# Moving small sums between engines in a fused layer: segment sums on TensorE, memory queries normalised at every step

## The chip, the cores and the metric

The kernel runs on one core of a Trainium2 chip. The metric is device time in microseconds. The kernel before takes 1494.43 us (median of three runs, 1494.37 to 1498.48). The profile describes one execution, whose span from first to last instruction is 1492.6 us; all times inside the kernel are counted from the start of that span.

A core has five engines that work side by side, each on its own queue of instructions: TensorE (PE: matrix products, whose weight loads are shown apart as PEld), VectorE (DVE), ScalarE (ACT), GpSimd (POOL) and SyncE (SP, used here to issue transfers). TensorE writes its products into PSUM; VectorE and ScalarE read them from there ("evict" them), and only then can TensorE use the same PSUM tile again.

## The reference

The input x is 2048 tokens of 1024 channels in bf16. After a layer norm it feeds two branches, whose sums with x are the output.

```python
# A: attention in 64 segments of 32 tokens, with 8 memory tokens carried along
for s in range(64):
    h = concat([mem, xn[32*s : 32*s + 32]])           # 40 tokens
    q, k, v = h @ Wq, h @ Wk, h @ Wv                  # 32 heads of 128
    p = softmax(where(mask, q @ k.T * scale, -1e9))
    o = (p @ v) @ Wo
    mem = o[:8]                                       # for the next segment
    out_A[s] = o[8:]
# B: mixing MLP
h  = gelu(layernorm(xn) @ w1)                         # 1024 x 1024
x1 = xn + shift(h) @ w2                               # tokens shifted by +-1, +-2
out_B = x1 + gelu(layernorm(x1) @ w3) @ w4            # 1024 -> 3584 -> 1024
out = x + out_A + out_B
```

The memory runs from segment to segment, which would make branch A serial. The kernel instead assumes that a memory query attends evenly to its 40 keys, so that the next memory follows from the **sum** of a segment's tokens. It computes these 64 segment sums early, sends them through Wv and Wo in advance, and then handles four blocks of 16 segments in parallel. Along the way it computes what the memory queries really yield, compares that with what it had assumed, and at the end runs a slow exact loop if they differ. With these inputs that loop isn't entered.

## The kernel before

The stages of the program, with the tile sizes: 16 tiles of 128 tokens; blocks ("tb" in the MLP, "b" in attention) of 512 tokens; 32 attention steps, each one block and four heads.

Statistics and first normalisation of a tile (VectorE and GpSimd), then transposes by TensorE or by a transposing transfer, then the product with w1:

```python
def ln_half(n, c):                       # c = 0, 1: half of the channels
    nc.vector.bn_stats(sts[n][:, c, :], xts[n][:, c*512:(c+1)*512])
    if c == 0: return
    nc.vector.bn_aggr(lnst[:, n, 0:2], sts.pop(n)[:])
    nc.vector.tensor_scalar(ab[:, 0:1], lnst[:, n, 1:2], EPS, None, op0=add)
    nc.vector.tensor_scalar(ab[:, 1:2], ab[:, 0:1], EPS, lnst[:, n, 1:2], op0=mult, op1=add)
    nc.gpsimd.tensor_tensor(lnst[:, n, 2:4], ab[:], neghalf[:], op=pow)
    ...                                  # loads of later x tiles
def ln_apply(n):
    nc.vector.tensor_scalar(xn2[:], xts[n][:], mean, rstd2, op0=subtract, op1=mult)
    ...
def normalise_x(n):                      # xts[n] becomes the normalised x, in place
    nc.scalar.activation(xts[n][:], xts[n][:], Identity, bias=..., scale=...)

warm(12); ln_stats(0); ln_half(1, 0); ln_apply(0); pe_trans(0)
ln_half(1, 1); w1_first(0, range(4)); ...
ln_half(2, 0); ln_apply(1); pe_trans(1)
...                                      # [cut] tiles 1 to 5
for g in range(2, 8):                    # pairs of tiles
    for n in (2*g + 2, 2*g + 3): ln_stats(n + 1); ln_apply(n); dma_trans(n)
    stage1(g, range(4))                  # 4 chains of 8 matmuls, 256 columns
    for n in (2*g, 2*g + 1): normalise_x(n)
    stage1(g, range(4, 8))
```

The MLP's second part, per block tb: 28 chains of 8 matmuls into h3T, then 4 tiles x 2 halves, each a chain of 28 matmuls and one VectorE eviction into R1. Between the chains a "filler" does the segment sums (blocks 0 and 1) and the products of the sums with 16 weight chunks (4 heads each; first Wv, then Wo):

```python
def make_xn(n):                          # normalised x to DRAM, 256 KB
    nc.sync.dma_start(xt[:], x_v[:, n, :])
    nc.vector.tensor_scalar(xt[:], xt[:], mean, rstd, op0=subtract, op1=mult)     # L455
    nc.gpsimd.dma_start(xn_v[:, n, :], xt[:])
def load_sum(b):                         # 512 tokens back, transposed
    nc.sync.dma_start_transpose(sums[b], xn_d[b*512:(b+1)*512, :])
def seg_sums(b, k0):
    nc.vector.tensor_reduce(xs[:, k0:k0+2, 16*b:16*b+16], sums[b]..., op=add)     # L463
plan[(1, 1, 2*i + 1)] = i                # chunk i after half 2i+1 of block 1, and so on
def load_R1(n):                          # residual of tile n
    nc.sync.dma_start(R1[:], R1_v[:, n, :]); nc.sync.dma_start(xt[:], x_v[:, n, :])
    nc.gpsimd.tensor_tensor(R1[:], R1[:], xt[:], op=add)

for tb in range(4):
    for f in range(28):
        ... 8 matmuls (L580), gelu by ScalarE; filler(tb, 0, f)
        if f == 20: load_R1(4*tb)
    for j in range(4):
        if j < 3: load_R1(4*tb + j + 1)
        for ch in range(2):
            ps = mm_tile("ps4")          # one of four PSUM tiles, in turn
            ... 28 matmuls (L596)
            nc.vector.tensor_tensor(R1[...], ps[:], R1[...], op=add)              # L597
            filler(tb, 1, 2*j + ch)
        nc.gpsimd.dma_start(R_v[:, n, :], R1[:])
        if tb == 3 and j == 0: att_prep()        # first attention weights, 4 MB
```

Attention: in step i TensorE makes queries, keys and values (4 chains each), the scores of step i-1 and the values of step i-2. The softmax runs on VectorE; column 32 of the scores is the memory query, whose probabilities are used unnormalised and divided once per block:

```python
def soft(s):
    ...                                  # 2 transposes, mask, sum, reciprocal, product (VectorE)
    nc.vector.transpose(s.PT[:, :, 0:SEG], Pn[:])                                 # L707
    nc.gpsimd.tensor_copy(s.PT[:, :, SEG:W], ET[:, :, SEG:W])                     # memory column
    ...
    nc.gpsimd.tensor_copy(EMs[s.b][...], ET[...][:, :, :, SEG])
def norm_sums(b):                        # once per block
    for j in range(4): nc.tensor.matmul(psN[:, j, :], qones[:, j, :], EM, ...)    # 128x128
    nc.vector.tensor_scalar(rm, psN, float(M), None, op0=add)
def norm_recip(b, j): nc.vector.reciprocal(rms[b][:, j, :], rms[b][:, j, :])
def norm_apply(b): nc.vector.tensor_tensor(o4, o4, rms[b]..., op=mult)
def norm_add(b):   nc.vector.tensor_tensor(oTs[b][:], oTs[b][:], VM[...], op=add)
def out_part(b, c, h0, h1, nsp=1):       # output chain: 32 matmuls per part, nsp equal parts
    ...
# end of the kernel
norm_sums(b); norm_recip x4; norm_apply(b); norm_add(b); compare(b); finite()
out_chain(b, 4); out_chain(b, 5); out_chain(b, 6); verdict(); out_part(b, 7, 0, 32, 2)
```

Of the kernel before, what the change touches and what calls it, by code (L numbers as in the profile page):

```python
# [29 lines left out]
H = 32  # L30
# [33 lines left out]
def kernel(  # L64
# [37 lines left out]
    def const_tile(name, arr, dt=BF16, later=False):  # L102
        a = _bf(arr) if dt == BF16 else np.asarray(arr, np.float32)
        d = nc.inline_tensor(a, name=name)
        t = cpool.tile(list(arr.shape), dt, name=name + "_sb")
        load = lambda: nc.gpsimd.dma_start(t[:], d.ap())
        if later:
            return load, t
        load()
        return t  # L110
# [36 lines left out]
    m0s = spec.tile([P, KT, 1], F32)  # L147
# [17 lines left out]
    with ExitStack() as keepx:  # L165
# [6 lines left out]
        with ExitStack() as p0:  # L172
# [29 lines left out]
            def ln_half(n, c):  # L202
                if c == 0:
                    sts[n] = ring.tile([P, 2, 6], F32, tag="st", name="st")
                nc.vector.bn_stats(sts[n][:, c, :], xts[n][:, c * 512:(c + 1) * 512])  # L205
                if c == 0:
                    return
                nc.vector.bn_aggr(lnst[:, n, 0:2], sts.pop(n)[:])
                ab = ring.tile([P, 2], F32, tag="ab", name="ab")
                nc.vector.tensor_scalar(ab[:, 0:1], lnst[:, n, 1:2], EPS, None, op0=ALU.add)  # L210
                nc.vector.tensor_scalar(ab[:, 1:2], ab[:, 0:1], EPS, lnst[:, n, 1:2], op0=ALU.mult, op1=ALU.add)
                nc.gpsimd.tensor_tensor(lnst[:, n, 2:4], ab[:], neghalf[:], op=ALU.pow)
                for t in {0: (3,), 1: (4, 5), 2: (6, 7)}.get(n, (n + 5,)):
                    if t < NT:
                        load_x(t)
# [9 lines left out]
            def ln_apply(n):  # L225
                g, j = divmod(n, 2)
                if j == 0:
                    xn2Ts[g] = ring.tile([P, 2, KT, P], BF16, tag="xn2T", name="xn2T", bufs=4)
                xn2 = xn2s[n] = ring.tile([P, D], BF16, tag="xn2", name="xn2", bufs=4)
                nc.vector.tensor_scalar(xn2[:], xts[n][:], lnst[:, n, 0:1], lnst[:, n, 3:4], op0=ALU.subtract, op1=ALU.mult)  # L230
                nms[n] = ring.tile([P, 1], F32, tag="nm", name="nm", bufs=8)
                nc.gpsimd.tensor_scalar(nms[n][:], lnst[:, n, 0:1], lnst[:, n, 2:3], -1.0, op0=ALU.mult, op1=ALU.mult)
# [14 lines left out]
            def pe_trans(n):  # L247
                xn2 = xn2s.pop(n)
                ps = [mm_tile("psT")[:], mm_tile("psT")[:]]
                for h in range(2):  # L250
                    p3_ = ps[h].rearrange("p (k t) -> p k t", k=4)
                    for k in range(4):
                        nc.tensor.matmul(p3_[:, k, :], xn2[:, (4 * h + k) * P:(4 * h + k + 1) * P], ident[:], start=True, stop=True)
                    for q in range(0, 4, 2 if n == 0 else 4):
                        w = 2 if n == 0 else 4
                        nc.scalar.copy(xn2Ts[n // 2][:, n % 2, 4 * h + q:4 * h + q + w, :], p3_[:, q:q + w, :])

# [42 lines left out]
            load_eye9()  # L300
# [19 lines left out]
            ln_stats(5)  # L320
            ln_apply(4)
            dma_trans(4)
            single(3, 0)
            normalise_x(2)
# [5 lines left out]
            for g in range(2, NT // 2):  # L330
# [7 lines left out]
                for n in (2 * g, 2 * g + 1):  # L338
                    normalise_x(n)
                stage1(g, range(4, KT))  # L340

# [5 lines left out]
        with ExitStack() as p2:  # L347
            ring = p2.enter_context(tc.tile_pool(name="p2ring", bufs=4))
            for n in range(NT):
# [23 lines left out]
                if n == 8:  # L373
                    load_qones()
                    load_causal()
                    load_mask40()

    attx = main.enter_context(ExitStack())
    with ExitStack() as p3:
# [12 lines left out]
        nc.vector.tensor_copy(m0s[:], ps9[:, :, M:M + 1])  # L392
# [49 lines left out]
        for i in range(4):  # L442
            plan[(1, 1, 2 * i + 1)] = i
            plan[(2, 0, 7 * i + 6)] = 4 + i
            plan[(2, 1, 2 * i + 1)] = 8 + i
            plan[(3, 0, 7 * i + 6)] = 12 + i
# [3 lines left out]
        sums = {}  # L450

        def make_xn(n):
            xt = ring.tile([P, D], BF16, tag="xt", name="xt", bufs=2)
            nc.sync.dma_start(xt[:], x_v[:, n, :])
            nc.vector.tensor_scalar(xt[:], xt[:], lnst[:, n, 0:1], lnst[:, n, 2:3], op0=ALU.subtract, op1=ALU.mult)  # L455
            nc.gpsimd.dma_start(xn_v[:, n, :], xt[:])

        def load_sum(b):
            sums[b] = x3_pool.tile([P, KT * 512], BF16, tag="x0", name=f"xTs{b}")
            nc.sync.dma_start_transpose(sums[b][:].rearrange("p (k t) -> p k t", k=KT), xn_d[b * 512:(b + 1) * 512, :])  # L460

        def seg_sums(b, k0):
            nc.vector.tensor_reduce(xs[:, k0:k0 + 2, 16 * b:16 * b + 16], sums[b][:].rearrange("p (k s i) -> p k s i", k=KT, i=SEG)[:, k0:k0 + 2, :, :], axis=AX.X, op=ALU.add)  # L463

        def last_sum():
            nc.vector.tensor_tensor(xb[:, :, 0:1], m0s[:], xs[:, :, 0:1], op=ALU.add)
            nc.vector.tensor_copy(xb[:, :, 1:NG], xs[:, :, 1:NG])
            load_chunk(0, 0)

        prep = {}  # L470

        def do(tb, ph, i, f, *a):
            prep.setdefault((tb, ph, i), []).append((f, a))

        for n in range(6):
            do(0, 0, 10 + 3 * n, make_xn, n)
        for n in range(6, 14):
            do(0, 1, n - 6, make_xn, n)
        do(1, 0, 0, make_xn, 14)
        do(1, 0, 3, make_xn, 15)  # L480
        for b, (load, sumat) in enumerate((((0, 1, 1), [(0, 1, 4)] * 4), ((0, 1, 5), [(1, 0, 1)] * 2 + [(1, 0, 2)] * 2),
                                           ((1, 0, 3), [(1, 0, 10 + t) for t in range(4)]), ((1, 0, 14), [(1, 0, 22 + t) for t in range(4)]))):
            do(*load, load_sum, b)
            for t, pos in enumerate(sumat):
                do(*pos, seg_sums, b, 2 * t)
        do(1, 0, 26, last_sum)

        def filler(tb, ph, i):
            for f, a in prep.get((tb, ph, i), ()):
                f(*a)  # L490
# [13 lines left out]
        def load_R1(n):  # L504
# [4 lines left out]
            nc.gpsimd.tensor_tensor(R1[:], R1[:], xt[:], op=ALU.add)  # L509
            R1s[n] = R1  # L510
# [47 lines left out]
        def att_prep():  # L558
# [14 lines left out]
            nc.gpsimd.memset(A["SS"][:], 0.0)  # L573

        for tb in range(4):
            for f in range(FT):
# [6 lines left out]
                if f == 20:  # L583
                    load_R1(tb * 4)
            if tb == 3:
                rightx.close()
                att_open()
# [30 lines left out]
    EMs = {}  # L618
# [6 lines left out]
    def new_step(i):  # L625
# [4 lines left out]
        if s.hg == 0:  # L630
            EMs[s.b] = smp.tile([P, NHG, 4, 4], BF16, tag="EM", bufs=2, name="EM")
# [64 lines left out]
    def soft(s):  # L696
# [11 lines left out]
        nc.gpsimd.tensor_copy(s.PT[:, :, SEG:W], ET[:, :, SEG:W])  # L708
# [4 lines left out]
        nc.gpsimd.tensor_copy(EMs[s.b][:, s.hg, :, :].rearrange("p h m -> p m h"), ET[:].rearrange("p (m h) i -> p m h i", h=4)[:, :, :, SEG])  # L713
# [77 lines left out]
    rms = {}  # L791

    def norm_sums(b):
        ps = mm_tile("psN")
        p3_ = ps[:].rearrange("p (j c) -> p j c", j=4)
        EM = EMs[b][:].rearrange("p g h m -> p (g h m)")
        for j in range(4):
            nc.tensor.matmul(p3_[:, j, :], qones[:, j, :], EM, start=True, stop=True)
        rm = smp.tile([P, 512], F32, tag="rm", name="rm")
        rms[b] = rm[:, 0:512].rearrange("p (j c) -> p j c", j=4)  # L800
        nc.vector.tensor_scalar(rms[b], p3_, float(M), None, op0=ALU.add)

    def norm_recip(b, j):
        nc.vector.reciprocal(rms[b][:, j, :], rms[b][:, j, :])

    def norm_apply(b):
        o4 = oTs[b][:].rearrange("p h (m j) -> p h m j", j=4)
        nc.vector.tensor_tensor(o4, o4, rms[b].rearrange("p j (h m) -> p h m j", m=4), op=ALU.mult)

    def norm_add(b):  # L810
# [39 lines left out]
    def out_part(b, c, h0, h1, nsp=1):  # L850
        m, ch = divmod(c, 2)
        w = 512 // nsp
        if h0 == 0:
            parts[b, c] = [mm_tile("psP") for _ in range(nsp)]
        for q in range(nsp):
            ps = parts[b, c][q]
            cc = slice(ch * 512 + q * w, ch * 512 + (q + 1) * w)
# [7 lines left out]
            nc.vector.tensor_tensor(ot[:, 0:w], ps[:, 0:w], Rt[:, q * w:(q + 1) * w], op=ALU.add)  # L865
# [24 lines left out]
    for i in range(NS):  # L890
# [29 lines left out]
        if s.hg == 2 and s.b > 0:  # L920
            at(2, norm_sums, s.b - 1)
            for j in range(4):
                at((4, 5, 7, 8)[j], norm_recip, s.b - 1, j)
            at(10, norm_apply, s.b - 1)
            at(11, norm_add, s.b - 1)
# [34 lines left out]
        if last:  # L960
# [17 lines left out]
            norm_sums(b)  # L978
            for j in range(4):
                norm_recip(b, j)  # L980
            norm_apply(b)
            norm_add(b)
# [6 lines left out]
            out_part(b, 7, 0, H, 2)  # L989
# [129 lines left out]
```

## Time and profile before

| stretch (us) | what runs there | length | TensorE busy | VectorE busy | ScalarE busy |
|---|---|---|---|---|---|
| 0 to 68.73 | layer norm, transposes, product with w1 | 68.73 | 63.34 | 36.55 | 44.78 |
| 68.73 to 124.36 | product with w2, second layer norm | 55.63 | 55.31 | 46.26 | 18.42 |
| 124.36 to 221.07 | MLP block 0 | 96.71 | 96.45 | 13.79 | 18.46 |
| 221.07 to 333.70 | MLP block 1 | 112.63 | 103.41 | 30.36 | 16.72 |
| 333.70 to 438.10 | MLP block 2 | 104.40 | 104.08 | 7.63 | 16.72 |
| 438.10 to 538.80 | MLP block 3 | 100.70 | 100.44 | 10.38 | 16.72 |
| 538.80 to 765.00 | attention, block 0 | 226.20 | 224.45 | 94.89 | 76.05 |
| 765.00 to 1492.60 | attention, blocks 1 to 3, and the end | 727.60 | 720.11 | 284.62 | 137.47 |

How to read it: the rows come from the busy times of each engine in windows of the trace. A row's length less the busy time of TensorE is the time in which TensorE did nothing. Some matmul records are missing, and in a long row they show as a little idle time. A line of the profile that is shown below names the engine, the line of the kernel (L597), the operation, what it wrote and read, the shape, how often it ran, and, in brackets, for how long the engine had been idle before it and what ended that. The granted clock is TensorE's, as a share of full speed.

### The profile page before, as it was taken

The numbers are of one execution on the slowest core, as the hardware profiler recorded it, in microseconds if no ns is written. First come the engines' busy times: TensorE is split into PE (matmuls) and PEld (weight loads), VectorE is DVE, ScalarE is ACT, GpSimd is POOL, SyncE is SP. The second block draws the span as 40 slices with busy tenths as digits, with TensorE's granted clock in tenths as the row PEclk, the third lists the DMA queues.
The fourth block names the chain that finished last, engine by engine and source line by source line (L and its number), as shares of the span: only waits on it lengthen the run. The fifth ranks groups of instructions, "written<-read, shape, count | busy, mean of one in ns | idle before, by whom it ended". The sixth has DMA issues, their size and how long they took to land.

```text
span 1492.6 us, 27953 instructions
## 1 busy us (share of the span) xinstructions
PE 1467.6 (98%) x12154; PEld 755.3 (51%) x12272; DVE 524.5 (35%) x1042; ACT 345.3 (23%) x871; POOL 205.7 (14%) x482
## 2 busy tenths in 40 slices
PE   8999997999999999999999999999999999999998
PEld 7844443444444456666544444444444444444444
DVE  8283034110000212445440355431264442163443
ACT  5633202203103013333320222220123220032220
POOL 6152131121211101121200000000000000000000
PEclk9999999999999999999999999999999999999999
DMA  8599765342542634565532364451245442244301
GB/s 218 138 266 226 280 216 151 118 153 96 191 149 99 212 113 157 183 190 180 184 114 64 94 174 150 143 169 49 83 142 171 155 156 72 67 142 147 123 12 62
DMA packets 207999, 216.77 MB, mean 145 GB/s; under 512 B 66936, under 2 KB 174600, under 8 KB 207872
## 3 DMA queue, kind: packets, MB, share of 16 engines
q1 hardware_dynamic: 199584, 187.21, 42.2%
q0 software_dynamic: 8288, 27.72, 5.4%
q8 instruction: 98, 1.61, 0.5%
q14 instruction: 29, 0.24, 0.1%
HBM read 174.26 MB, written 25.17 MB: 134 GB/s over the span
## 4 chain that ended last, share of the span: by engine, by line
PE 94%; DMA 2%; DVE 2%; issue 1%; SPq 1%; POOL 0%; DVEq 0%; POOLq 0%
PE psK L659 15%; PE psP L859 15%; PE psV L668 15%; PE psQ L641 15%; PE ps L580 13%; PE ps L596 11%; PE ps L356 4%; PE ps L260 2%; PE psS L692 1%; PE psO L722 1%; PE psM L677 1%; DMA xt<-in_A_x_dram 1%; DVE st L205 1%; PE psvb L414 1%; PE psG L435 1%
## 5 line engine op out<-in xcount | busy, mean ns | idle before, releaser
L859 PE MATMUL psP<-wo_sb,oX 128*128 128x512 bf16 (+1 forms) x1035 | 221.1, 372 | 1.1
L596 PE MATMUL ps<-w,hT_all 128*128 128x512 bf16 x874 | 193.7, 379 | 1.2
L659 PEld LDWEIGHTS <-w 128*128 128x128 bf16 x1280 | 125.1, 98 | 99.1
L641 PE MATMUL psQ<-xT,w 128*128 128x512 bf16 x744 | 169.1, 379 | 1.3
L668 PE MATMUL psV<-w,xT 128*128 128x512 bf16 x744 | 169.0, 379 | 1.3
L659 PE MATMUL psK<-xT,w 128*128 128x512 bf16 x763 | 169.4, 379 | 0.3
L859 PEld LDWEIGHTS <-oX 128*128 128x128 bf16 x1056 | 103.1, 98 | 117.2
L641 PEld LDWEIGHTS <-w 128*128 128x128 bf16 x1024 | 98.7, 98 | 116.0
L660 ACT CAST K<-psK 128x512 bf16<-128x512 f32 (+1 forms) x160 | 80.2, 501 | 303.8 <-PE psK L659 302.8
L648 DVE TENSOR_TENSOR Q<-psQ,QM 128x512 bf16<-128x512 f32 (+1 forms) x128 | 87.2, 685 | 166.0 <-PE psQ L641 107.5
L669 ACT CAST V<-psV 128x512 bf16<-128x512 f32 x128 | 74.8, 584 | 289.7 <-PE psV L668 289.6
L596 PEld LDWEIGHTS <-hT_all 128*128 128x128 bf16 x896 | 87.2, 98 | 103.8
L581 ACT ACTIVATE hT_all<-ps 128x512 bf16<-128x512 f32 x112 | 66.7, 597 | 294.9 <-PE ps L580 294.9
L668 PEld LDWEIGHTS <-xT 128*128 128x128 bf16 x768 | 74.1, 98 | 84.7
L580 PE MATMUL ps<-xn3T,w3a 128*128 128x512 bf16 x448 | 100.9, 387 | 8.9 <-DVE R L597 8.9
L580 PE MATMUL ps<-xn3T,w3b 128*128 128x512 bf16 x448 | 97.7, 379 | 0.0
L727 DVE TENSOR_TENSOR oX<-psE,VM 128x128 bf16<-128x128 f32 x32 | 9.3, 291 | 215.3 <-PE psE L723 215.3
L734 DVE TENSOR_TENSOR oX<-psO,VM 128x96 bf16<-128x96 f32 (+2 forms) x256 | 82.0, 391 | 0.0
L865 DVE TENSOR_TENSOR ot<-psP,Rt 128x512 bf16<-128x512 f32 (+1 forms) x33 | 22.3, 675 | 167.7 <-PE psP L859 164.9
L580 PEld LDWEIGHTS <-w3a 128*128 128x128 bf16 x448 | 44.1, 99 | 63.2 <-issue 13.3
L597 DVE TENSOR_TENSOR R<-ps,R 128x512 f32<-128x512 f32 x32 | 22.0, 689 | 137.8 <-PE ps L596 137.2
L580 PEld LDWEIGHTS <-w3b 128*128 128x128 bf16 x448 | 43.6, 98 | 51.9
(160 smaller groups left out, 1252.4 us busy)
## 6 DMA issues: line engine op xcount, KB each, us to landing
w<-in_A_Wq_dram SPq DMA_DIRECT2D x32, 1024.0 KB, 5.4
w<-in_A_Wk_dram SPq DMA_DIRECT2D x32, 1024.0 KB, 5.5
w<-in_A_Wv_dram SPq DMA_DIRECT2D x32, 1024.0 KB, 6.4
R_scratch<-x POOLq DMA_DIRECT2D x16, 512.0 KB, 9.0
xt<-in_A_x_dram SPq DMA_DIRECT2D x32, 256.0 KB, 3.8
R<-R_scratch SPq DMA_DIRECT2D x16, 512.0 KB, 6.4
R_scratch<-R POOLq DMA_DIRECT2D x16, 512.0 KB, 6.4
chunk<-in_A_Wv_dram SPq DMA_DIRECT2D x8, 1024.0 KB, 5.6
```

Of the source, the lines that this page charges most:

```text
L356: nc.tensor.matmul(ps[:], hTB[:, k, o:o + P], w2_sb[:, k, ch * 512:(ch + 1) * 512], start=(k == 0), stop=(k == KT - 1))
L580: nc.tensor.matmul(ps[:], w3[:, k, (f % FH) * P:(f % FH + 1) * P], xn3Ts[tb][:, :, k, :], start=(k == 0), stop=(k == KT - 1))
L581: nc.scalar.activation(h3T[:, f, :], ps[:], ACTF.Gelu_apprx_tanh)
L596: nc.tensor.matmul(ps[:], h3T[:, f, j * P:(j + 1) * P], w4t[f // 4][:, f % 4, ch * 512:(ch + 1) * 512], start=(f == 0), stop=(f == FT - 1))
L641: nc.tensor.matmul(ps[:], w[:, k, hh * P:(hh + 1) * P], s.xm[:, k, 0:512], start=(k == 0), stop=(k == KT - 1))
L648: nc.vector.tensor_tensor(q3[:, j0:16, 0:SEG], p3_[:, j0:16, :], QM[:, 4 * s.hg + hh, z + j0:z + 16].unsqueeze(2).to_broadcast((P, 16 - j0 ...
L659: nc.tensor.matmul(ps[:, 0:c], w[:, k, hh * P:(hh + 1) * P], s.xm[:, k, h2 * c:(h2 + 1) * c], start=(k == 0), stop=(k == KT - 1))
L660: nc.scalar.copy(s.K[:, hh, h2 * c:(h2 + 1) * c], ps[:, 0:c])
L668: nc.tensor.matmul(ps[:], s.xm[:, k, m * P:(m + 1) * P], w[:, k, :], start=(k == 0), stop=(k == KT - 1))
L669: nc.scalar.copy(s.V[:, m, :], ps[:])
L734: nc.vector.tensor_tensor(oX[:, h0:h0 + hn, :].rearrange("p h (m c) -> p m h c", c=P)[:, m0:m1, :, SEG * j:SEG * (j + 1)], o4[:, 4 * m0:4 ...
L859: nc.tensor.matmul(ps[:, 0:w], oX[:, h, m * P:(m + 1) * P], wo_sb[:, h, cc], start=(h == 0), stop=(h == H - 1))
```

## The change

Five things are moved.

1. **Segment sums** are made by TensorE in the first stage, straight from the normalised tiles in SBUF: the tile is the weight, and a constant of 128x4 (which token belongs to which of the tile's four segments) is the moving operand, eight matmuls of four columns a tile. ScalarE copies the result. This replaces the sums by VectorE from a transposed copy read back from DRAM. The normalised x that attention reads from DRAM is now made in the residual's load, from the x that is loaded there anyway. The products with the weight chunks move earlier by half a block.
2. **Memory queries** are normalised in every step: their 16 probabilities per partition are transposed so that their sum lies along the free axis, summed, divided, transposed back and put into the probabilities that the values are multiplied with. The sums by TensorE and the divisions once per block fall away.
3. **Tile 0** is normalised in two pieces, of 256 and 768 channels, so that its transposes may start after the first; the two statistics operations no longer depend on each other; tile 4 is normalised between the two halves of tile 5's statistics.
4. **Constants** that are needed late are loaded by SyncE in the second stage instead of GpSimd.
5. **The last output chain** is cut into 384 and 128 columns instead of 256 and 256.

```diff
-                nc.vector.tensor_scalar(ab[:, 1:2], ab[:, 0:1], EPS, lnst[:, n, 1:2], op0=ALU.mult, op1=ALU.add)
+                nc.vector.tensor_scalar(ab[:, 1:2], lnst[:, n, 1:2], 1.0 + EPS, EPS * EPS, op0=ALU.mult, op1=ALU.add)
...
-                nc.vector.tensor_scalar(xn2[:], xts[n][:], lnst[:, n, 0:1], lnst[:, n, 3:4], ...)
+                for c0, c1 in (((0, 256), (256, D)) if n == 0 else ((0, D),)):
+                    nc.vector.tensor_scalar(xn2[:, c0:c1], xts[n][:, c0:c1], lnst[:, n, 0:1], lnst[:, n, 3:4], ...)
...
+            def seg_sums(n):
+                ps = aux_tile([P, KT, 4], "AB"[n % 2], "psX")
+                for k in range(KT):
+                    nc.tensor.matmul(ps[:, k, :], xts[n][:, k * P:(k + 1) * P], segone[:], start=True, stop=True)
+                nc.scalar.copy(xs[:, :, 4 * n:4 * n + 4], ps[:])
...
-            ln_stats(5)
+            ln_half(5, 0)
             ln_apply(4)
+            ln_half(5, 1)
             dma_trans(4)
             single(3, 0)
+            seg_sums(0)
+            seg_sums(1)
...
                 for n in (2 * g, 2 * g + 1):
+                    seg_sums(n - 2)
                     normalise_x(n)
                 stage1(g, range(4, KT))
+            seg_sums(NT - 2)
+            seg_sums(NT - 1)
...
-            plan[(1, 1, 2 * i + 1)] = i          # and (2, 0, ..), (2, 1, ..), (3, 0, ..)
+            plan[(0, 1, 2 * i + 1)] = i          # and (1, 0, ..), (1, 1, ..), (2, 0, ..)
...
-        def make_xn(n): ...                      # and load_sum, seg_sums, last_sum, with their places
...
         def load_R1(n):
             nc.gpsimd.tensor_tensor(R1[:], R1[:], xt[:], op=ALU.add)
+            nc.vector.tensor_scalar(xt[:], xt[:], lnst[:, n, 0:1], lnst[:, n, 2:3], op0=ALU.subtract, op1=ALU.mult)
+            nc.gpsimd.dma_start(xn_v[:, n, :], xt[:])
...
+            if tb == 0:
+                load_chunk(0, 0)                 # after the 28 chains of block 0
...
-        nc.gpsimd.tensor_copy(s.PT[:, :, SEG:W], ET[:, :, SEG:W])
+        nc.gpsimd.tensor_copy(MQ[:, 0:16], ET[:, :, SEG])
+        nc.vector.transpose(mt[:], MQ[:])
+        nc.vector.tensor_reduce(sm[:, 0:1], mt[:], axis=AX.X, op=ALU.add)
+        nc.vector.tensor_scalar(sm[:, 0:1], sm[:, 0:1], float(M), None, op0=ALU.add)
+        nc.vector.reciprocal(sm[:, 1:2], sm[:, 0:1])
+        nc.vector.tensor_scalar(MP[:], mt[:], sm[:, 1:2], None, op0=ALU.mult)
+        nc.vector.transpose(MT[:], MP[:])
+        nc.gpsimd.tensor_copy(s.PT[:, :, SEG], MT[:, 0:16])
...
-        # norm_sums, norm_recip, norm_apply, norm_add
+    def mem_add(b):
         nc.vector.tensor_tensor(oTs[b][:], oTs[b][:], VM[:, :, 7 + 16 * b:23 + 16 * b], op=ALU.add)
...
-            out_part(b, 7, 0, H, 2)
+            out_part(b, 7, 0, H, (384,))
```

## The prediction

> **What bounds the kernel now.** I read the page first, then who waits for whom on TensorE, then TensorE's and VectorE's instructions in order of time around the longest waits, then the windows by stage, and last the groups by shape for the price of one instruction.
>
> From part 1 of the page:
>
> ```profile
> PE 1467.6 (98%) x12154; PEld 755.3 (51%) x12272; DVE 524.5 (35%) x1042; ACT 345.3 (23%) x871; POOL 205.7 (14%) x482
> ```
>
> TensorE is busy for all but 25.0 us of the 1492.6 us span, and no other engine comes near. So a change can win in two ways only: shorten TensorE's own work, or close its holes. The waits of TensorE say where the holes are (us in total, times, longest):
>
> ```profile
> PE ps L580 <- DVE R L597: 8.9, 2, 5.0
> PE psT L253 <- DVE xn L230: 2.0, 2, 1.4
> PE ps L260 <- DMA xn2T<-xn: 1.6, 2, 1.2
> PE psO L722 <- issue: 0.6, 1, 0.6
> ```
>
> The attention stages have one hole of 0.6 us in 954 us, so there is nothing to close there. The large hole is 8.9 us where the MLP passes from its first to its second block of 512 tokens: two matmuls of the first product wait for a PSUM bank that VectorE has not yet emptied (the eviction into R). TensorE's own instructions there (start, length):
>
> ```profile
> 221.07 1.89 PE L580 MATMUL ps<-xn3T,w3a 128*128 128x512 bf16 x8
> 226.87 5.01 PE L580 MATMUL ps<-xn3T,w3a 128*128 128x512 bf16 x16 [3.92 <-DVE R L597]
> 236.87 9.44 PE L580 MATMUL ps<-xn3T,w3a 128*128 128x512 bf16 x36 [4.99 <-DVE R L597]
> ```
>
> And VectorE in the same stretch:
>
> ```profile
> 219.93 1.79 DVE L455 TENSOR_SCALAR xt<-xt,lnst 128x1024 bf16<-128x1024 bf16 x1 [5.73 <-DMA xt<-in_A_x_dram]
> 221.64 4.58 DVE L463 TENSOR_REDUCE xs<-xTs 128x32 f32<-128x1024 bf16 x4
> 226.14 0.68 DVE L597 TENSOR_TENSOR R<-ps,R 128x512 f32<-128x512 f32 x1
> ...
> 235.67 0.55 DVE L455 TENSOR_SCALAR xt<-xt,lnst 128x1024 bf16<-128x1024 bf16 x1 [7.80 <-DMA xt<-in_A_x_dram]
> 236.13 0.68 DVE L597 TENSOR_TENSOR R<-ps,R 128x512 f32<-128x512 f32 x1
> ```
>
> VectorE is not short of time; it stands in line. An eviction that TensorE needs (L597) lies behind a normalisation that waits 5.7 and 7.8 us for its transfer, and behind four segment sums of 1.2 us each. The windows give the second price of the hole. Columns: stretch, its length, then busy time of each engine, the granted clock, the DMA share:
>
> ```profile
> 124.36:172.72 48.36, 48.36 (x227) 21.93 (x225) 2.67 (x7) 17.87 (x29) 2.02 (x6) 1.00 0.97 262
> 226.80:231.90 5.10, 5.01 (x16) 1.87 (x16) 1.07 (x3) 0.60 (x1) 1.07 (x2) 0.71 1.03 220
> 236.87:243.00 6.13, 6.13 (x22) 2.53 (x22) 0.58 (x2) 1.19 (x2) 1.25 (x3) 0.75 0.78 257
> ```
>
> After each wait the clock is 0.71 and 0.75 for a while, which costs 0.29 x 5.10 + 0.25 x 6.13 = 3.0 us more. Check: the first product of block 0 takes 48.36 us (first row); that of block 1 runs from 221.07 to 281.55, that is 60.48. The excess is 12.1 us, and 8.9 + 3.0 = 11.9 explains it.
>
> [...]
> - [...] waits of 3.92 and 4.99 us are each followed by about 3 us lost as above, while the waits under 1.5 us in the first stage have no dip.
> - [...] for forty columns: four of them (psZO, L787) take 0.26 us with a mean of 180 ns for one, so the other three follow at (260 - 180)/3 = 27 ns.
> - [...]
> - [...] The trace has 153 ns for a one-element TENSOR_SCALAR and 253 ns for a reciprocal of 16.
>
> **The change part by part.**
>
> *Segment sums leave VectorE and the second MLP stage.* Removed: sixteen normalisations L455, sixteen sums L463 (18.4 us of VectorE), four transposing loads, sixteen second loads of x. The normalised x is now made from the x that the residual load fetches anyway. With nothing waiting on a late transfer ahead of the evictions at the end of block 0, the hole and its clock dip go: I take the measured excess, **-12.1 us**.
>
> *Segment sums come to TensorE.* Added in the first stage: 16 tiles x 8 matmuls = 128 matmuls of four columns. At the 26 to 27 ns of the forty-column ones that is 128 x 0.026 = +3.3 us of TensorE. With each tile goes one ScalarE copy of 128x32, about 0.19 us (the 128x32 cast L647 has 186 ns); ScalarE has room: in the steady part (33.80 to 68.73) it is busy 24.41 of 34.93 us. The first four tiles' matmuls, 32 x 0.026 = 0.8 us, fall before the two waits for the transposed tiles (0.42 us at 25.42 and 1.22 us at 33.80), so they fill holes. The transposes start a little earlier too: the pair of statistics operations no longer depend on one another, so the second need not wait for the first (0.19 us start to start now, about 0.09 where two neighbours are independent, as L824 and L837 late in the kernel), and tile 4 is normalised half a statistics step (0.68 us) sooner. I let the start of tiles 6 and 7 move from 33.80 to about 33.0: -0.8. The other twelve tiles pay in full: 12 x 8 x 0.026 = +2.5. Sum for this stage **+1.7 us**.
>
> *Tile 0 in two pieces.* The first transposes can start about 0.2 us sooner and the first products perhaps 0.3 us sooner. But the next thing on TensorE, the transposes of tile 1 at 10.53, follows a normalisation at 9.94 that stands behind statistics which started at 9.33, when tile 2's x landed. That transfer is not touched. The gain becomes a longer wait: **0**.
>
> *Memory queries normalised per step.* Removed: four 128x128 sums per block on TensorE; the last block's lie between 1460.26 and the next matmul at 1460.48, 0.22 us, so 4 x 0.22 = **-0.9 us**; on VectorE the reciprocals (16 x 0.91), 4 x 0.68 and 4 x 1.05 = 21.5 us. Added per step on VectorE: two transposes of 128x32 (about 0.20 each, an estimate on the line from 301 ns for 128 columns to 712 for 512), a reduction, three small operations at 0.15 to 0.17: about 1.05 us busy, 1.3 with gaps, so some 42 us in 32 steps. It lies off the path. In a normal step the softmax ends well before the next queries' first eviction. In the first block it is tightest: the last transpose L707 starts 610.26 and ends 610.97, and the next query eviction begins at 613.43, after 2.46 us idle. 1.3 fits: 0. At the end, the probabilities are ready at 1439.4 (1438.99 + 0.41) and used at 1444.09: 1.6 us later still fits.
>
> *Last chain in 384 and 128 columns.* TensorE's time is the same (512 columns in all). The last addition covers 128 columns instead of 256: 0.29 us (L727's shape, 291 ns) for 0.42. The transfer is half as large, with little to gain: **-0.15 us**.
>
> *Constants on SyncE, earlier use of the weight chunks.* Small issues taken from GpSimd; the chunk products move by half a block and are as many as before: 0.
>
> Sum: -12.1 + 1.7 + 0 - 0.9 - 0.15 = -11.45; 1494.43 - 11.45 = **1483.0 us**.
>
> **The rivals.**
> - *TensorE pays for the weights.* Each four-column matmul needs a new 128x128 weight load of 98 ns. Were these not overlapped, 128 x 0.098 = 12.5 us would eat the whole gain: about 1492. Against it: 71-column products with new weights each (L677) take 19.1 us for 512, 37 ns each, so loads overlap.
> - *A new line at VectorE's door.* The normalisation now stands behind GpSimd's addition (2.12 us) and in front of the evictions of the tile before. It is worst in the last block, where that load lies behind 4 MB of attention weights: its addition ends at 514.45, and an eviction that ran at 508.56 would move to about 515. With four PSUM banks TensorE needs that one again three chains later (evictions are 6.0 us apart: 508.56, 514.54, 520.64, 526.63), at about 526, so I expect no hole. If I am wrong, one to two holes of 4 us with a clock dip each come back: 1489 to 1494.
> - *Attention is delayed by the six small operations.* If each of 32 steps lost 0.5 us, 1499. The single hole in attention speaks against it.
> - *The start gains after all*, if tile 2's transfer comes sooner: another -0.5 us, 1482.5.
>
> **Range and chances.** The largest term is a measured excess and firm to about 1 us. The first stage is open by about 2 us upwards (weight loads, copies behind ScalarE's 1.24 us normalisations) and 1 downwards; a small new wait in the MLP or attention could cost 2. Range 1480.5 to 1486.5. Two per cent is 29.9 us, more than all of TensorE's idle time, so faster by 2% needs something I don't see: 0.01. Slower by 2% needs a loss in every attention step: 0.01. Within 2%: 0.98.
>
> **What would show it.** Right: no wait of TensorE on R at the start of the second block, a first product of 48.4 us there, clock 1.00; 128 new matmuls at 26 to 30 ns in the first stage, which ends near 70.4 instead of 68.73; the transposes of tile 1 still near 10.5; attention steps unchanged but for the missing sums. Wrong: waits of TensorE on R or on the queries' eviction, a first stage longer by more than 4 us, or new holes at the first chunk products, whose chunk is now loaded as the first block's second product begins.

## The result, and the profile after

The kernel after takes 1484.61 us (median of 4 runs, 1483.74 to 1485.59). The ratio to the runs of before, taken beside it, is 0.9932 (95% interval 0.9909 to 0.9954). The forecast was 1483.0 us with a range of 1480.5 to 1486.5.

The profiled span fell from 1492.6 to 1483.8 us, by 8.8 us, where the working had 11.45. Part 1 of the page, with the same columns as before:

```profile
PE 1466.9 (99%) x12266; PEld 755.8 (51%) x12384; DVE 513.4 (35%) x1194; ACT 346.5 (23%) x887; POOL 204.7 (14%) x479
```

TensorE was busy almost as long as before (1467.6): its idle time fell from 25.0 to 16.9 us. So 8.1 of the 8.8 us were idle time. In the busy time the terms nearly cancel: 3.0 us of slow matmuls after the waits and 0.9 us of query sums went, 3.2 us of segment sums came. The waits of TensorE after, from 0.5 us up and without that for the warm-up's constant (us in total, times, longest):

```profile
PE psT L253 <- DVE xn L230: 1.5, 2, 0.8
PE psO L708 <- POOL PT L695: 0.9, 1, 0.9
PE psO L708 <- issue: 0.6, 1, 0.6
PE ps L281 <- DMA w_sb<-in_B_w_dram: 0.5, 2, 0.3
```

The 8.9 us on R are gone, as are the 1.6 us on transposed tiles. A wait of 0.9 us on PT is new. MLP block 1 on TensorE, in order of time (start, length):

```profile
226.18 1.12 PE L425 MATMUL psvb<-xb,chunk 128*128 128x63 bf16 x32
227.14 12.25 PE L556 MATMUL ps<-xn3T,w3a 128*128 128x512 bf16 x56
239.23 1.12 PE L425 MATMUL psvb<-xb,chunk 128*128 128x63 bf16 x32
240.18 12.25 PE L556 MATMUL ps<-xn3T,w3a 128*128 128x512 bf16 x56
```

Nothing is in brackets, so there is no wait, and 56 matmuls take 12.25 us, as those of the second product before them do (12.25 us from 214.09). The chunk products between them are the ones that were moved. They moved by a whole block of the MLP, not by half a block as said above: the first runs at 187.05 us and ran at 293.63 before. The window over that first product has the clock at 1.00:

```profile
227.14:279.31 52.17, 52.17 (x358) 25.77 (x355) 2.23 (x5) 16.72 (x28) 10.56 (x23) 1.00 0.34 111
```

52.17 us less four chunk products of 0.96 us (227.14 - 226.18) is 48.3: the 48.36 us of block 0 before.

Where the 8.8 us came from and went, by the starts of the same instructions in both traces:

| stretch, first instruction to first instruction | before | after | difference |
|---|---|---|---|
| start to the transposes of tile 2 | 15.46 | 16.44 | +1.0 |
| from there to the product with w2 | 53.27 | 54.54 | +1.3 |
| product with w2 to the first queries of attention | 470.85 | 458.71 | -12.1 |
| first queries to the values of the last step | 904.51 | 905.11 | +0.6 |
| from there to the last matmul | 44.43 | 44.26 | -0.2 |
| last matmul to the end | 4.08 | 4.77 | +0.7 |

### The profile page after: what moved, and what is told of

It reads as the page before. It is cut to its first block, busy times and chain, and to the rows that moved or that the text cites. A ratio compares the mean times of both kernels' runs of the same rounds, so it can differ in the third digit from the quotient of the medians.

```text
span 1483.8 us, 28316 instructions
## 1 busy us (share of the span) xinstructions
PE 1466.9 (99%) x12266; PEld 755.8 (51%) x12384; DVE 513.4 (35%) x1194; ACT 346.5 (23%) x887; POOL 204.7 (14%) x479
## 4 chain that ended last, share of the span: by engine, by line
PE 98%; DVE 1%; issue 1%; DMA 0%; SPq 0%; ACT 0%; POOL 0%; POOLq 0%; DVEq 0%
PE psK L635 15%; PE psP L827 15%; PE psQ L617 15%; PE psV L644 14%; PE ps L556 13%; PE ps L574 13%; PE ps L367 4%; PE ps L266 3%; PE psS L668 1%; PE psO L708 1%; PE psM L653 1%; PE psvb L425 1%; PE psG L446 1%; PE ps L295 0%; DMA x<-in_A_x_dram 0%
## 5 line engine op out<-in xcount | busy, mean ns | idle before, releaser
L827 PE MATMUL psP<-wo_sb,oX 128*128 128x512 bf16 (+2 forms) x1035 | 221.0, 372 | 1.1
L556 PE MATMUL ps<-xn3T,w3a 128*128 128x512 bf16 x448 | 97.7, 379 | 0.0
L833 DVE TENSOR_TENSOR ot<-psP,Rt 128x512 bf16<-128x512 f32 (+2 forms) x33 | 22.3, 675 | 168.9 <-PE psP L827 166.1
L481 DVE TENSOR_SCALAR xt<-xt,lnst 128x1024 bf16<-128x1024 bf16 x16 | 8.7, 546 | 179.3 <-POOL R L480 179.3
```

The source lines that it names most:

```text
L556: nc.tensor.matmul(ps[:], w3[:, k, (f % FH) * P:(f % FH + 1) * P], xn3Ts[tb][:, :, k, :], start=(k == 0), stop=(k == KT - 1))
L827: nc.tensor.matmul(ps[:, 0:w], oX[:, h, m * P:(m + 1) * P], wo_sb[:, h, cc], start=(h == 0), stop=(h == H - 1))
```

## The experiments

The first question was whether the line in front of VectorE's evictions explains the -12.1; the next, where 2.7 us of the forecast went; the last, whether the pieces add up to something better.

### Segment sums alone, and queries alone

*e1* is the kernel before with part 1 only; *e2* is the kernel before with part 2 only.

```diff
  # e1: before, with
+ seg_sums(n) by TensorE in the first stage; plan a block earlier
+ load_R1: normalise xt and store it
- make_xn, load_sum, seg_sums (VectorE), last_sum
  # e2: before, with
+ soft(): memory column transposed, summed, divided, transposed back
- norm_sums, norm_recip, norm_apply
```

> The kernel before with part 1 alone (segment sums on TensorE, normalised x made in the residual's load, chunks half a block earlier). Theory (evictions stood in line behind late transfers and sums on VectorE): no wait of TensorE on R, clock 1.00 through block 1, attention starts about 10 us earlier than before, first stage 1.5 to 2.3 us longer; about 1484.5 us. Rival (the gain comes from the queries' normalisation in attention): within 1 us of before, 1494.

> The kernel before with part 2 alone (memory queries normalised per step). Theory: four times 0.22 us of TensorE saved, but 0.9 us lost at the last step, where the values of step 30 wait for its memory column; the wait of 8.9 us on R stays; sum about 0, 1494.4 us. Rival (part 2 carries the gain): 1485 to 1490.

e1: 1484.83 us, ratio 0.995 (0.994 to 0.9961). No wait on R, no dip in block 1. e2: 1492.69 us, ratio 1.0007 (0.9992 to 1.0021). So part 1 carries the gain. Part 2 shows none, but e2's interval, from 1.2 us faster to 3.1 us slower, is too wide to exclude a gain of 0.9 us. Both theories held, except that e2's wait on R was smaller than expected. It shows how the hole looks on another execution. First its waits, then TensorE at the start of block 1:

```profile
PE ps L583 <- DVE R L600: 5.2, 1, 5.2
PE ps L260 <- DMA xn2T<-xn: 2.4, 1, 2.4
PE psW L198 <- DVE fill L177: 1.5, 1, 1.5
PE psO L733 <- POOL PT L720: 0.9, 1, 0.9
```

```profile
222.67 5.34 PE L583 MATMUL ps<-xn3T,w3a 128*128 128x512 bf16 x24
233.21 11.97 PE L583 MATMUL ps<-xn3T,w3a 128*128 128x512 bf16 x43 [5.19 <-DVE R L600]
```

The same code for this stage now has one wait of 5.2 us where the profile of before had two of 3.9 and 5.0. From the product with w2 to the first queries of attention e2 takes 466.61 us and the kernel before 470.85, while all twelve profiles without this hole take 458.71 or 458.72. So the hole cost 7.9 us in one execution and 12.1 in the other. That its size depends on when transfers land is a guess, not shown here. A size that varies would fit the scatter of the runs of before: 39 of them beside e1 and e2 go from 1482.97 to 1497.19 us, the 20 of e2, which keeps the hole, from 1488.54 to 1496.94, the 20 of e1 from 1483.39 to 1486.39. But this hole isn't the only source of scatter: single runs of e9, e11 and e12 below took 1497.97, 1495.27 and 1491.30 us, though their profiles have no wait on R. Those three runs had a mean granted clock of 0.995 to 0.998; what happened in them isn't known.

### Was it the sums or the transfers?

*e7* leaves the sums on VectorE and only moves them, with the transposing loads of later blocks, to where ScalarE does the evictions.

```diff
- b0: load (0,1,1), sums (0,1,4) x4      b1: load (0,1,5), sums (1,0,1) x2, (1,0,2) x2
- b2: load (1,0,3), sums (1,0,10..13)    b3: load (1,0,14), sums (1,0,22..25)
+ b0: load (0,1,1), sums (1,0,4) x2, (1,0,5) x2
+ b1: load (1,0,5), sums (1,0,9) x2, (1,0,10) x2
+ b2: load (1,0,11), sums (1,0,15..18)   b3: load (1,0,18), sums (1,0,22..25)
```

> The kernel before with the segment sums kept on VectorE, but all of them, and the transposing loads of blocks 1 to 3, moved into the first product of block 1, where ScalarE evicts. Theory A (the four sums in front of the evictions and the loads behind them make the line): both waits on R and the clock dips go, about 12 us less, 1482.5. Theory B (the normalisations' late transfers alone make it): waits on R of 4 us and more remain, 1490 or more.

1484.38 us, ratio 0.9938 (0.9915 to 0.9961): as much as the whole change, without a single sum on TensorE. VectorE in e7 around the start of block 1 (223.95):

```profile
217.92 1.49 DVE L455 TENSOR_SCALAR xt<-xt,lnst 128x1024 bf16<-128x1024 bf16 x1 [5.65 <-DMA xt<-in_A_x_dram]
219.33 0.68 DVE L597 TENSOR_TENSOR R<-ps,R 128x512 f32<-128x512 f32 x1
222.02 0.55 DVE L455 TENSOR_SCALAR xt<-xt,lnst 128x1024 bf16<-128x1024 bf16 x1 [2.02 <-DMA xt<-in_A_x_dram]
222.48 0.68 DVE L597 TENSOR_TENSOR R<-ps,R 128x512 f32<-128x512 f32 x1
...
237.04 4.59 DVE L463 TENSOR_REDUCE xs<-xTs 128x32 f32<-128x1024 bf16 x4
```

The normalisations still wait for their transfers, but never long enough to make TensorE wait; the 4.6 us of sums lie at 237, where no eviction stands behind them. From the product with w2 to the first queries e7 takes 458.72 us, within 0.01 us of the kernel after. So VectorE had the time for the sums; it was their place in its queue, and that of the transposing loads in SyncE's, that cost the 12 us. Which of the two mattered more isn't separated, as e7 moves both.

### What a sum costs TensorE

*e8* does each of the 128 matmuls twice.

```diff
-                for k in range(KT):
+                for k in [*range(KT), *range(KT)]:
                     nc.tensor.matmul(ps[:, k, :], xts[n][:, k * P:(k + 1) * P], segone[:], start=True, stop=True)
```

> The kernel after with every segment-sum matmul done twice. Theory (25 ns each, weight loads overlapped): 128 more matmuls cost 3.2 us, all in the first stage. Rival (98 ns weight loads not overlapped, or ScalarE's copies bind): 5 us or more.

e8 took 1487.41 us in a single run. From the transposes of tile 2 to the product with w2 it takes 57.71 us, the kernel after 54.54. The lines of the stretches, with the same columns as the windows above, e8 first:

```profile
15.27:72.98 57.71, 57.71 (x812) 53.39 (x810) 24.89 (x72) 43.03 (x91) 18.60 (x33) 1.00 0.76 158
```

```profile
16.44:70.98 54.54, 54.54 (x684) 50.13 (x681) 24.13 (x71) 41.44 (x90) 18.47 (x32) 1.00 0.70 166
```

3.17 us for 128 matmuls is 24.8 ns each, near the 27 ns that the prediction read off the forty-column ones. A new 128x128 weight load each time (96 ns each in the kernel after) doesn't show. Both stretches are without idle time, so these sums are paid in full.

### The last step

In the last step of the kernel after, TensorE's values of step 30 follow directly on the scores of step 31. GpSimd writes the memory column that they read:

```profile
1421.32 0.21 DVE L694 STREAM_TRANSPOSE MT<-MP 128x32 bf16<-128x32 bf16 x1
1421.69 0.25 POOL L695 COPY PT<-MT 128x16 bf16<-128x16 bf16 x1 [7.99 <-DVE MT L694]
1421.99 0.62 PE L708 MATMUL psO<-PT,V 32*128 32x33 bf16 x60 [0.92 <-POOL PT L695]
```

*e5* puts other work in between:

```diff
             scores(s)
+            out_part(b, 0, 0, 8)
             values(p)
             soft(s)
-            out_part(b, 0, 0, hp)
+            out_part(b, 0, 8, hp)
```

> The kernel after with 8 of the 28 first matmuls of the last block's output moved ahead of the values of step 30. Theory (those values wait for the memory column, which comes at the end of a longer chain on VectorE and GpSimd): the wait of 0.92 us on PT goes, no new one comes, span 0.9 us shorter, 1482.9. Rival (the work behind has to wait for it anyway): a wait of the same size at the values of step 31.

The values of step 30 in e5:

```profile
1423.20 0.62 PE L708 MATMUL psO<-PT,V 32*128 32x33 bf16 x60
```

The wait on PT is gone and none replaces it: from the first queries to the values of step 31 it is 904.11 us instead of 905.11. (1485.28 us in a single run: its start was 0.1 us later than that of the kernel after, and it waited a little more in the first stage.)

### The last chain

*e3* ends in 256 and 256 columns: `out_part(b, 7, 0, H, (256,))`. *e12* is e9 below with 256, 128 and 128: `(256, 384)`.

> The kernel after with the last chain in 256 and 256 columns. Theory (rows of 256 bytes land later than rows of 512): from the end of the last addition to the end of the span 3.35 us as before instead of 4.2; the last addition 0.42 us instead of 0.29; span about 0.7 us shorter, 1483.1. Rival (the later end is chance): still about 4.2.

> As e9, with the last chain in 256, 128 and 128 columns. Theory (in the 384 and 128 cut the last transfer is late because a fetch of instructions occupies one transfer engine when it starts, not because its rows have 256 bytes): if the fetch falls elsewhere, the last transfer lands in 1.5 us and the end comes 0.13 us sooner than in e9. Rival (rows of 256 bytes are slow): landing again 2.4 us, end 0.8 us later than in e9.

In e3 (1484.71 us in a single run) the end comes 3.35 us after the last addition; after has 4.22. The transfers from the end of the last addition on; of after, then of e3 (KB each, us from issue to landing):

```profile
q1 hardware_dynamic: 144, 0.03, 10.1%
q8 instruction: 1, 0.02, 4.1%
issues: line engine op xcount, KB each, median us to landing
out_dram<-ot SPq DMA_DIRECT2D x1, 32.0 KB, 2.4
```

```profile
q1 hardware_dynamic: 144, 0.07, 16.3%
issues: line engine op xcount, KB each, median us to landing
out_dram<-ot SPq DMA_DIRECT2D x1, 64.0 KB, 1.5
```

Half the data lands 0.9 us later. In all seven kernels that end in 128 columns the end came 4.1 to 4.4 us after the last addition; in the seven that end in 256, six times 3.34 to 3.35 and once 4.04 (e1, whose transfer landed after 1.6 us all the same). The rows of 256 bytes, where e3 has 512, are one candidate; no run here shows their effect by itself. The other stands in the first fence: a packet of instructions (the q8 line) runs beside it, and none does in e3. e12 was to tell them apart, but there the packet came again (and the landing was 2.4 again, the end 4.13).

The times of the single packets narrow it. In the kernel after, 135 of the 144 packets of this transfer had started 1.13 us after the addition. The other nine, a sixteenth, started only at 1.34 to 1.45 us, after the packet of instructions had ended (at 1.13), and the last ended at 1.52; in e3 the last ended at 1.22. So the instructions fit as the cause of some 0.3 of the 0.9 us. The other 0.6 us pass between the last packet and the landing, and their cause stays open.

### The start

*e4* normalises tile 0 in one piece; *e6* loads tile 3's x later: `{0: (), 1: (3, 4, 5), ...}` for `{0: (3,), 1: (4, 5), ...}`.

> The kernel after with tile 0 normalised in one piece. Theory (the start is set by tile 2's x and by w1, which share the transfer engines with loads that now start 0.28 us earlier): statistics of tile 2 still start near 9.7, transposes of tile 2 still near 16.4; same time within 0.3 us. Rival (the split itself delays the start): they return to 9.33 and 15.40, 1.0 us faster.

> The kernel after with the load of tile 3's x issued with those of tiles 4 and 5 instead of after tile 0's statistics. Theory (that load takes transfer time from tile 2's x and w1): statistics of tile 2 start by 9.3 instead of 9.71, transposes of tile 2 by 15.5 instead of 16.44, span about 1 us shorter. Rival (landing times at the start vary by chance): no such order, 9.3 to 9.8 as in the others.

The statistics of tile 2 began at 8.51 us in e4 and at 8.44 in e6, and the transposes of tile 2 at 14.64 and 14.56, nearly 2 us before those of the kernel after (single runs: 1483.85 and 1483.76 us). In the kernel after, and in e6, VectorE at that point:

```profile
9.71 0.69 DVE L204 BATCH_NORM_STATS2 st<-x 128x6 f32<-128x512 bf16 x1 [1.70 <-DMA x<-in_A_x_dram]
10.32 0.53 DVE L230 TENSOR_SCALAR xn<-x,lnst 128x1024 bf16<-128x1024 bf16 x1
```

```profile
8.44 0.69 DVE L204 BATCH_NORM_STATS2 st<-x 128x6 f32<-128x512 bf16 x1 [0.35 <-DMA x<-in_A_x_dram]
9.04 0.53 DVE L230 TENSOR_SCALAR xn<-x,lnst 128x1024 bf16<-128x1024 bf16 x1
```

It looked as if e6 had the cause. It hadn't: e9, e10 and e12, with the same late load, began at 10.14, 9.60 and 9.28. The landing of tile 2's x moves by 1.7 us from profile to profile. With tile 0 in one piece the six profiles have 8.51, 8.51, 8.72, 9.06, 9.33 and 9.60; in two pieces the eight have 8.44, 9.15, 9.28, 9.66, 9.71, 9.73, 9.86 and 10.14.

This landing doesn't set the start alone. In ten profiles the transposes of tile 2 start 6.1 to 6.2 us after those statistics; in the kernel after, e3, e5 and e11 it is 6.7, since TensorE's weight loads wait there for w1. Before, then after:

```profile
10.94 4.51 PEld L275 LDWEIGHTS <-w_sb 128*128 128x128 bf16 x80
```

```profile
11.96 4.47 PEld L281 LDWEIGHTS <-w_sb 128*128 128x128 bf16 x80 [0.60 <-DMA w_sb<-in_B_w_dram]
```

These four are among the five profiles that have both the two pieces and the early load of tile 3's x (the fifth is e8); none of the other nine has the wait there. In the five, the transposes of tile 2 start at 15.27 to 16.54 us; with tile 0 in one piece at 14.64 to 15.72; with two pieces and the late load at 14.56, 15.41 and 16.26. So the two pieces bring no gain, and beside the early load they seem to cost about 1 us. That the loads are in each other's way there fits, but wasn't shown.

### All repairs together

*e9* is the kernel after with e3, e5 and e6. *e10* has tile 0 in one piece and the constants on GpSimd as before, the sums late on VectorE (e7) with part 2, the two independent statistics operations, tile 4 early, e5 and e6, and ends in 256 columns. *e11* is the kernel after again.

> The kernel after with the three repairs together: 8 output matmuls ahead of the values of step 30, the load of tile 3's x with those of tiles 4 and 5, the last chain in 256 and 256. Theory (the three losses are separate and all on TensorE's path): 1.0 + 1.0 + 0.9 us less than after, about 1481.8 us. Rival (what is gained at the start and in attention comes back as waits): within 0.5 us of after.

> Segment sums on VectorE, but late as in e7, with the queries per step, the two independent statistics operations, tile 4 early, and the three repairs of e9. Theory (the 128 matmuls of the sums are TensorE time that can be saved, and the transposed tiles come in time): first stage 2.5 to 3 us shorter than e9, about 1479.2 us. Rival (without the sums' matmuls TensorE waits for the transposed tiles 6 and 7 as before, 1.2 to 2.6 us and a clock dip): 1481 to 1483.

> The kernel after once more, for comparison on the same chip and as one more sample of the start. Theory (tile 2's x lands late when tile 3's load starts beside it in this order): statistics of tile 2 at 9.2 or later; 1484.6 us. Rival (chance): anything from 8.4 to 9.9.

| kernel | forecast us | median us | runs, lowest to highest | ratio to before (95%) |
|---|---|---|---|---|
| e11 (after again) | 1484.6 | 1485.57 | 17, 1483.83 to 1495.27 | 0.9948 (0.9936 to 0.9961) |
| e9 | 1481.8 | 1483.51 | 22, 1482.12 to 1497.97 | 0.9935 (0.9923 to 0.9948) |
| e10 | 1479.2 | 1483.47 | 6, 1481.61 to 1485.68 | 0.9937 (0.9918 to 0.9955) |
| e12 | as e9 | 1484.84 | 9, 1482.62 to 1491.30 | 0.9944 (0.9923 to 0.9965) |

e9 and e10 have medians 2 us below the kernel after. The intervals overlap, but all four were measured beside the same runs of before, so the runs can be compared directly: of the pairs of one run of e9 and one of e11, e9's is the lower in 81%, and the medians differ by 2.06 us (0.7 to 2.6 when the runs are resampled). So e9's repairs gain something; for e10, with six runs, and e12 this isn't shown. Neither e9 nor e10 reached its forecast. In e10 TensorE worked 51.69 us in its first stage instead of 54.54, but waited again:

```profile
15.70:68.87 53.17, 51.69 (x556) 46.91 (x554) 24.98 (x72) 39.85 (x75) 18.65 (x34) 1.00 0.79 171
```

```profile
PE ps L260 <- DMA xn2T<-xn: 1.4, 1, 1.4
```

Half of the 2.85 us saved came back as a wait for the transposed tiles: the rival's wait at 1.4 us, without the dip. e9, with its sums on TensorE, waited 1.1 us for them too.

Over all profiles: from the transposes of tile 2 to the product with w2, the four without sums on TensorE took 53.15 (e10), 53.27 (before), 55.58 (e2) and 56.42 us (e7), each with waits of 1.4 to 2.6 us for transposed tiles. Nine with the sums, done once, took 54.54 to 55.76 us; only e9 (1.1) and e5 (0.2) waited for those tiles. So the sums fill this hole as a rule, and against the longer two of the four they cost next to nothing.

## Why the prediction was right or wrong

The time lay in the range, and the mechanism of the main term was the one forecast. That the sum came out so near is partly luck: the forecast took the hole of one execution, 12.1 us, and another has 7.9. Measured again with more runs (e11), the whole change is worth 5.8 to 9.6 us, not 11.45, and part 1 alone (e1) 5.8 to 9.0 us, where -12.1 + 1.7 = -10.4 was forecast. Term by term, between the two profiles:

- **The hole at block 1, -12.1.** Measured -12.1, without wait or dip. The reading that the hole is a line in a queue, not a lack of VectorE time, is what e7 shows. What the working didn't see is that this term varies: it called the excess firm to about 1 us, and e2 has 7.9. One reading of it is wrong without harm to the sum: the waits are not "each followed by about 3 us lost". Each is followed by about 1.5 us lost; the 3.0 us are both.
- **The first stage, +1.7.** Measured +1.3 from the transposes of tile 2 on. The sums cost 24.8 ns each (e8), against 26, so 3.2 us; the two waits for transposed tiles closed completely (1.6 us), of which the working had filled 0.8 and let 0.8 be won by earlier transposes. The profile of before had the second shortest first stage of the four without sums on TensorE, so this term too depends on the execution.
- **Tile 0, 0.** The step was right that the split gains nothing while tile 2's x lands no sooner. It took that landing as fixed at 9.33 us; it came at 9.71 in the profile of after. This is 0.4 of the 1.0 us by which the start was later. The other 0.6 is the weight loads' wait for w1, which the working didn't consider.
- **The queries, -0.9.** This step failed. The working asked only whether the values of step 31 would wait ("the probabilities are ready at 1439.4 (1438.99 + 0.41) and used at 1444.09"). The values of step 30 follow their softmax within the same step there. The last transpose of that softmax and these values, before:

```profile
1429.88 0.71 DVE L707 STREAM_TRANSPOSE PT<-Pn 128x512 bf16<-128x512 bf16 x1
1431.29 0.62 PE L722 MATMUL psO<-PT,V 32*128 32x33 bf16 x60
```

Some 0.7 us were free where 1.6 were needed. The wait was 0.92 us; e5 removes it. In the other steps these values run a step later, with room to spare. The saving itself is there. From the first queries to the values of step 31 the three profiles without part 2 take 904.51 to 904.64 us, the seven with it 904.77 to 905.13, the four with it and with e5's order 903.96 to 904.25: 0.5 us saved on average, where 0.66 were expected for three blocks. The last block's 0.2 us come on top.

- **The last chain, -0.15.** Wrong in sign. The addition is shorter as said (0.29 for 0.42 us), but the transfer behind it landed later: last matmul to end +0.7. The working let half the bytes be no slower.
- **The rivals.** The sums' weight loads add nothing that shows (24.8 ns a matmul, where a load takes 96). The line at VectorE's door in the last MLP block made no hole (458.71 or 458.72 us from the product with w2 to the first queries, in every profile without the hole at block 1). The six operations of the softmax cost nothing that the totals above show inside a block. The start didn't gain.

The misses are +1.0 (start), -0.4 (first stage), +1.3 (queries: forecast -0.9, measured +0.6 - 0.2) and +0.8 (end), together +2.7: what was measured (11.45 - 8.8).

## What to carry to other kernels

Look at what stands in front of an eviction in its engine's queue before asking whether the engine has time: moving four sums by a few chains, and the transposing loads with them, was worth as much here (e7, 1484.38 us) as moving the sums to another engine (1484.61). Check the slack of a dependency in the last iteration by itself, since what runs a step later in the loop runs at once in its tail. Before a single transfer's landing or a single hole becomes a term of a sum, see it in more than one profile.

## What was not expected of the hardware

TensorE's clock also fell after waits well short of the 3.92 and 4.99 us of the first profile. In e2 a wait of 2.38 us in the first stage (31.54 to 33.93) was followed by this; columns as in the windows above, the clock third from the end:

```profile
32.00:34.00 2.00, 0.07 (x1) 0.10 (x2) 1.90 (x6) 0.00 (x0) 1.46 (x3) 0.89 1.13 264
34.00:36.00 2.00, 2.00 (x10) 1.36 (x11) 1.90 (x7) 0.17 (x1) 0.87 (x3) 0.50 1.03 361
36.00:38.00 2.00, 2.00 (x16) 1.61 (x14) 1.90 (x6) 0.59 (x2) 0.85 (x3) 0.75 1.35 269
```

In e7 a wait of 2.60 us (to 35.02) was followed by a clock of 0.67 from 35 to 37 us, 0.50 from 37 to 39 and 0.98 from 39 to 41. If the clock was either full or half, these shares put the start of e7's half clock at 35.68 us, 0.7 us after the wait had ended, and its length at about 3.4 us in both. The waits of 1.42 us in e10 and of 1.22 us in the kernel before had none after them (clock 1.00 over 15.70 to 68.87 us in e10, and over 33.80 to 40.00 before). So a dip came after a wait of 2.38 us and none after one of 1.42; what lies between isn't shown.
